# Rows of decay powers from one column by TensorE, first masks from the landed table, and a new order of low parts and conversions

## The chip, the cores and the metric

One core of one Trainium2 chip runs one program. The metric is the device time of one execution in microseconds (us). A trace by the hardware profiler belongs to one execution. Its engines are called PE (TensorE, the matrix products; PEld is its loading of weights), DVE (VectorE), ACT (ScalarE), POOL (GpSimd) and SP (SyncE, which issues most loads and stores).

## What is computed

Retention (attention with a decay) over 2 sequences of 768 positions with 8 heads of width 64, and behind it two feed-forward layers on 1536 tokens of width 512:

```python
Dmask = np.where(rel >= 0, lam[:, None, None] ** rel[None, :, :], 0.0)
lam_pow = lam[:, None, None] ** (pos[None, :, None] + 1)
for b in range(nb):
    intra = np.einsum('bhic,bhjc->bhij', qb, kb) * Dmask[None]
    intra = np.einsum('bhij,bhjd->bhid', intra, vb)
    inter = np.einsum('bhid,bhde->bhie', qb * lam_pow[None], kv_state)
    out[:, :, sl] = intra + inter
    kb_dec = kb * rev_pow[None]
    kv_state = lam_block[None, :, None, None] * kv_state + np.einsum('bhsd,bhse->bhde', kb_dec, vb)
# then, on the tokens:
x = np.maximum(x @ w_in, 0.0) ** 2 @ w_out
x = (1.0 / (1.0 + np.exp(-(x @ w_gate))) * (x @ w_val)) @ moe2_w_out
```

## The kernel before

The kernel works in chunks of 128 positions: chunks 0 to 5 are the first sequence, 6 to 11 the second, and a pair (c, c + 6) goes through the attention together. The order of the work on every engine is written out by hand (`tc.manual_schedule()`): each engine runs its instructions in the order of the program and waits where an operand or a buffer is not ready.

**The start.** `powers()` (L212) loads lam, makes the exponents `ex`, and POOL raises lam to them: `W` holds lam^1 to lam^128, one power a partition. `W` and zeros go to a table in memory, and `decay_table()` (L245) reads it back shifted by one row a partition, which gives every head's mask; its numbers lie eight apart. `warm_up(n)` (L268) issues n products that nothing uses. `state_decay()` (L232) picks the last power of each head into `G`, `decay_rows()` (L256) picks a row of the mask table for `L`, which scales queries; both by selecting products on TensorE with the matrix `E`. ScalarE and VectorE copy the table into `D` (L888, L889).

**The lead** (L898). For a pair: scores (L301, into two banks of PSUM a chunk; `sc`), the product of scores with the mask (L335, `at`, VectorE), keys and queries scaled by POOL (L322 `kd`, L310 `qd`), the new state's products (L368, `uv`), the output from within the chunk (L385) and from the state (L396), the update of the state `S` (L415, VectorE), its decay for the next pair (L352, ScalarE), and the output's copy or its split into a high and a low part (L425, L426). Four pairs go through the lead; the last two are put into slots of the following loop (`attend`, L810). The loads of q and k (`qk`), k and v (`kv`) and raw weights (`raw`) are issued by SP in the order of `FIRST`, `NEXT` and `LOOP`.

**The loop** `step_1(f)` (L828), f = 0 to 15, is the first layer on the first 512 tokens. TensorE does `stage_a(1, f)` (L457) and, a step later, `stage_b` (L471). Each weight comes as raw bits. It is converted in two operations on ScalarE (`conv_act`, L156 and L157) and three on VectorE (`conv_dve`: L179, L182, L174), of which the second reads the result of the first and the third that of the second. Then it is split into a high part (`whi`, ScalarE, L443) and a low part (`wlo`, VectorE, L445). `stage_a` needs the high part first and the low part from its fifth product on. The activations are split the same way (L498, L500). `weave(a, b)` issues two lists by turns, and `run` issues one. In most steps two weights are converted. Towards the loop's end `combine_x` and `combine_a` put more work on VectorE and ScalarE, for the products that follow it. Behind the loop come the rest of the first layer and the second layer; the change does not touch them.

Of the kernel before, what the change touches and what calls it, by code (L numbers as in the profile page):

```python
# [7 lines left out]
F32 = mybir.dt.float32  # L8
# [4 lines left out]
P = 128  # L13
CH = 128
TB = 512
WARM = 44
FILL = (72, 24)
# [22 lines left out]
def retention_moe_kernel(  # L40
# [40 lines left out]
    def bank():  # L81
        return ps.tile([P, 512], F32, tag="p", name="p")
# [120 lines left out]
    E = const.tile([P, 64], F32, name="E")  # L203
    G = [const.tile([P, 4, 1], F32, name=f"G{i}", tag=f"G{i}") for i in range(2)]
# [3 lines left out]
    L = [const.tile([P, 4, CH], F32, name=f"L{i}", tag=f"L{i}") for i in range(2)]  # L208
    S = [const.tile([P, 4, 64], F32, name=f"S{i}", tag=f"S{i}") for i in range(2)]
    w_dram = dram.tile([256, H], F32, name="w_dram")  # L210

    def powers():  # L212


        src = bass.AP(lam.tensor, lam.offset, [[0, P], [1, H]])
        nc.sync.dma_start(out=lam8, in_=src)
        nc.vector.memset(warm, 0.0)
        nc.gpsimd.iota(row, pattern=[[1, 1]], base=0, channel_multiplier=1)
        nc.vector.memset(Z[:, 0 : 127 * H], 0.0)
        nc.vector.memset(Z[:, 127 * H :], 1.0)  # L220
        nc.vector.tensor_scalar(out=ex, in0=row, scalar1=1.0, scalar2=None, op0=ALU.add)
        nc.vector.tensor_scalar(
            out=E, in0=row.to_broadcast([P, 64]), scalar1=127.0, scalar2=None, op0=ALU.is_equal
        )
        nc.scalar.dma_start(out=w_dram[0:128], in_=Z)
        nc.scalar.copy(ex, ex)
        nc.gpsimd.tensor_tensor(
            out=W[:, :, 0], in0=lam8, in1=ex.to_broadcast([P, H]), op=ALU.pow
        )
        nc.scalar.dma_start(out=w_dram[128:256], in_=W[:, :, 0])  # L230

    def state_decay():  # L232


        t = bank()
        w = W.rearrange("a (p r) o -> a r (p o)", r=2)
        for s in range(2):
            for g in range(2):
                nc.tensor.matmul(
                    t[64 * g : 64 * g + 64, 4 * s : 4 * s + 4], lhsT=E[64:128],  # L240
                    rhs=w[64:128, g ^ s], start=True, stop=True, skip_group_check=True,
                )
            nc.vector.tensor_copy(G[s][:, :, 0], t[:, 4 * s : 4 * s + 4])
# [11 lines left out]

    def decay_rows():  # L256


        for s in range(2):
            t = bank()  # L260
            for g in range(2):
                nc.tensor.matmul(
                    t[64 * g : 64 * g + 64], lhsT=E[64:128],
                    rhs=D[64:128, g ^ s].rearrange("a p i -> a (p i)"), start=True, stop=True,
                )
            nc.scalar.copy(L[s].rearrange("a p i -> a (p i)"), t)
# [47 lines left out]
    def att_prep(c):  # L314
        s, n = divmod(c, SEQ_CH)
        sc = sc_t.pop(c)
        at_t[c] = double("at")
        dst = [pv(at_t[c][:, g, :]) for g in range(2)]
        kn = kv_t[c][:, 0, :]
        if n < SEQ_CH - 1:  # L320
            kd = kd_t[c] = unit("kd")
            nc.gpsimd.tensor_tensor(  # L322
                out=kd.rearrange("s (h d) -> s h d", h=H),
                in0=kn.rearrange("s (h d) -> s h d", h=H),
                in1=W.to_broadcast([P, H, 64]), op=ALU.mult,
            )
        qt = qk_t.pop(c)[:, 0, :]
        if c == NCH - 1:
            query(NCH, qk_t.pop(NCH)[:, 0, :])
        elif c > SEQ_CH:  # L330
            query(c + 1, qk_t[c + 1][:, 0, :])
        elif 0 < n:
            query(c, qt)
        return [
            lambda g=g: nc.vector.tensor_tensor(  # L335
                out=dst[g], in0=pv(sc[g]), in1=D[:, g ^ s], op=ALU.mult
            )
            for g in range(2)
        ]
# [33 lines left out]
    def att_out(pair):  # L373
# [4 lines left out]
        for c in pair:  # L378
            s = c // SEQ_CH
            v = kv_t.pop(c)[:, 1, :].rearrange("s (h d) -> s h d", h=H)  # L380
# [22 lines left out]
        for c in pair:  # L403
            o_t[c] = uv_t.pop(c, None), ov[c]

    def att_state(c):
        s = S[c // SEQ_CH]
        uv, _ = o_t[c]
# [9 lines left out]
    def att_x(c):  # L418
        _, ov = o_t.pop(c)
# [390 lines left out]
    def attend(half):  # L810
# [7 lines left out]
        if what == "out":  # L818
# [4 lines left out]
            att_out(pair)  # L823
            passed(REST)
# [3 lines left out]
    def step_1(f):  # L828
# [3 lines left out]
        weave(conv_dve() if n > 0 else [], split_w(1, f + 1) if f + 1 < NF1 else [])  # L832
# [7 lines left out]
        weave(conv_dve() if n > 1 else [], ops)  # L840
# [31 lines left out]
    with tc.manual_schedule():  # L872
# [4 lines left out]
        state_decay()  # L877
# [10 lines left out]
        nc.scalar.copy(D[:, 0], table[:, 0])  # L888
        nc.vector.tensor_copy(D[:, 1], table[:, 1])  # L889
        ops = [op for c in PAIRS[0] for op in att_prep(c)]  # L890
        att_uv(PAIRS[0])
        warm_up(FILL[1])
        decay_rows()
        query(SEQ_CH + 1, qk_t[SEQ_CH + 1][:, 0, :])
        run(ops)
        for c in PAIRS[1]:
            att_scores(c)
        for k in range(LEAD):  # L898
# [3 lines left out]
            att_out(pair)  # L902
            if k + 2 < LEAD:
                for c in PAIRS[k + 2]:
                    att_scores(c)
# [12 lines left out]
            else:  # L918
                att_scores(PAIRS[LEAD][0])
                for c in pair:  # L920
                    run(att_state(c))
                run([f for c in pair for f in att_x(c)])
                weave(split_w(1, 0), ops)
# [106 lines left out]
```

## Time and profile before

| | us |
|---|---|
| median of 3 runs (lowest, highest) | 600.98 (599.19, 603.05) |
| the profiled execution: its time, its span | 600.89, 599.1 |
| busy in the span: PE, DVE, ACT, POOL | 583.8, 436.2, 339.6, 29.4 |

The span is the time from the first to the last instruction in the trace; around it lie 1.8 us. A wait stands in square brackets behind an instruction: how long its engine was idle and what it waited for. Matrix products overlap, so the distance from start to start tells more than a duration. [...]

### The profile page before, as it was taken

The numbers are of one execution on the slowest core, as the hardware profiler recorded it, in microseconds if no ns is written. First come the engines' busy times: TensorE is split into PE (matmuls) and PEld (weight loads), VectorE is DVE, ScalarE is ACT, GpSimd is POOL, SyncE is SP. The second block draws the span as 40 slices with busy tenths as digits, with TensorE's granted clock in tenths as the row PEclk, the third lists the DMA queues.
The fourth block names the chain that finished last, engine by engine and source line by source line (L and its number), as shares of the span: only waits on it lengthen the run. The fifth ranks groups of instructions, "written<-read, shape, count | busy, mean of one in ns | idle before, by whom it ended". The sixth has DMA issues, their size and how long they took to land.

```text
span 599.1 us, 8743 instructions
## 1 busy us (share of the span) xinstructions
PE 583.8 (97%) x3188; PEld 480.1 (80%) x3188; DVE 436.2 (73%) x676; ACT 339.6 (57%) x557; POOL 29.4 (5%) x29
## 2 busy tenths in 40 slices
PE   7898999998999999999999999999999999999997
PEld 7686778886788888888888888888888888888885
DVE  4359998899888868898977788694768676569101
ACT  3358888998656456666567654544454454537001
POOL 2471100000000000000000000000000000000000
PEclk9699999999999999999999999999999999999999
DMA  8995797793145376999988954511332422659003
GB/s 269 412 408 197 260 295 280 257 320 118 63 120 204 107 253 254 383 412 411 394 332 277 316 175 165 174 39 55 121 106 105 141 79 82 208 193 353 0 1 141
DMA packets 52157, 126.94 MB, mean 212 GB/s; under 512 B 5777, under 2 KB 6033, under 8 KB 52114
## 3 DMA queue, kind: packets, MB, share of 16 engines
q1 hardware_dynamic: 51024, 124.41, 57.9%
q10 hardware_dynamic: 1090, 1.97, 1.0%
q8 instruction: 25, 0.41, 0.3%
q14 instruction: 18, 0.15, 0.1%
HBM read 90.71 MB, written 35.66 MB: 211 GB/s over the span
## 4 chain that ended last, share of the span: by engine, by line
PE 82%; DVE 8%; ACT 4%; issue 3%; DMA 2%; POOL 0%; SPq 0%; ACTq 0%; DVEq 0%; POOLq 0%
PE p L623 30%; PE p L773 25%; PE p L457 13%; PE p L471 8%; PE p L301 2%; PE p L385 2%; DVE u L174 1%; DVE m L182 1%; DMA kv<-in_kv 1%; DVE t L556 1%; DMA a<-w 1%; DVE xcl L545 1%; PE p L396 1%; DVE m L179 1%; PE p L368 1%
## 5 line engine op out<-in xcount | busy, mean ns | idle before, releaser
L623 PE MATMUL p<-xch,ah 128*128 128x512 f32 x280 | 109.6, 392 | 0.2 <-DVE c L637 0.2
L623 PE MATMUL p<-xch,al 128*128 128x512 f32 x280 | 109.0, 389 | 0.0
L623 PE MATMUL p<-xcl,ah 128*128 128x512 f32 x280 | 109.0, 389 | 0.0
L773 PE MATMUL p<-g2h,whi 128*128 128x512 f32 x224 | 87.2, 389 | 0.0
L773 PE MATMUL p<-g2h,wlo 128*128 128x512 f32 x224 | 87.2, 389 | 0.0
L773 PE MATMUL p<-g2l,whi 128*128 128x512 f32 x224 | 87.2, 389 | 0.0
L623 PEld LDWEIGHTS p<-xch,ah 128*128 128x128 f32 x280 | 52.6, 188 | 13.1 <-ACT s L632 1.7
L623 PEld LDWEIGHTS p<-xch,al 128*128 128x128 f32 x280 | 52.6, 188 | 11.1
L637 DVE TENSOR_TENSOR c<-p,s 128x512 f32<-128x512 f32 x60 | 41.2, 688 | 27.5 <-PE p L623 21.0
L623 PEld LDWEIGHTS p<-xcl,ah 128*128 128x128 f32 x280 | 52.6, 188 | 10.7
L632 ACT COPY s<-p 128x512 f32<-128x512 f32 x60 | 35.2, 587 | 37.8 <-PE p L623 37.5
L156 ACT ACTIVATE j<-raw 128x512 f32<-128x512 f32 x68 | 45.8, 673 | 18.2 <-DMA raw<-in_w 10.4
L445 DVE TENSOR_TENSOR wlo<-u,whi 128x512 fp32r<-128x512 f32 x68 | 46.0, 704 | 7.3 <-ACT whi L443 6.0
L174 DVE CUSTOM_DVE_ANT_0 u<-m,r 128x1024 uint16<-128x1024 uint16 x68 | 48.6, 715 | 3.1
L773 PEld LDWEIGHTS p<-g2h,wlo 128*128 128x128 f32 x224 | 42.1, 188 | 8.8
L773 PEld LDWEIGHTS p<-g2h,whi 128*128 128x128 f32 x224 | 42.1, 188 | 8.7
L773 PEld LDWEIGHTS p<-g2l,whi 128*128 128x128 f32 x224 | 42.1, 188 | 8.7
L182 DVE SCALAR_TENSOR_TENSOR m<-j,m 128x512 int32<-128x512 int32 x68 | 47.9, 704 | 1.3
L457 PE MATMUL p<-xh,wlo 128*128 128x512 f32 x160 | 43.3, 393 | 4.8 <-DVE wlo L445 4.8
L157 ACT ACTIVATE r<-raw 128x512 int32<-128x512 uint32 x68 | 45.2, 664 | 4.5 <-PE p L471 2.9
L443 ACT CAST whi<-u 128x512 fp32r<-128x512 f32 x68 | 39.2, 617 | 12.2 <-DVE u L174 11.7
L457 PE MATMUL p<-xh,whi 128*128 128x512 f32 x160 | 43.1, 391 | 0.7 <-ACT whi L443 0.7
(98 smaller groups left out, 899.5 us busy)
## 6 DMA issues: line engine op xcount, KB each, us to landing
raw<-in_w SPq DMA_DIRECT2D x68, 512.0 KB, 7.0
w<-u SPq DMA_DIRECT2D x68, 256.0 KB, 4.0
u<-w SPq DMA_DIRECT2D x64, 256.0 KB, 5.0
g<-g SPq DMA_DIRECT2D x56, 256.0 KB, 4.3
g<-g SPq DMA_DIRECT2D x28, 512.0 KB, 7.7
a<-w SPq DMA_DIRECT2D x20, 512.0 KB, 4.0
kv<-in_kv SPq DMA_DIRECT2D x12, 512.0 KB, 9.2
qk<-in_qk SPq DMA_DIRECT2D x10, 512.0 KB, 8.7
```

The lines of the kernel that those rows point to most:

```text
L156: nc.scalar.activation(j, t[:, :, 1].bitcast(F32), AF.Copy, scale=2.0**-112)
L157: nc.scalar.activation(r, t[:, :, 0].bitcast(mybir.dt.uint32), AF.Copy, scale=2.0**-29)
L174: nc.vector.tensor_tensor(out=w.bitcast(I32), in0=m, in1=r, op=ALU.add)
L182: lambda: nc.vector.scalar_tensor_tensor(out=m, in0=j, scalar=-(2**31), in1=m, op0=ALU.bitwise_and, op1=ALU.bitwise_or),
L443: nc.scalar.copy(hi, src)
L445: lambda lo=lo, src=src, hi=hi: nc.vector.tensor_tensor(out=lo, in0=src, in1=hi, op=ALU.subtract)
L457: nc.tensor.matmul(acc, lhsT=a[:, kk * P : (kk + 1) * P], rhs=b[:, kk, :], start=i == 0, stop=i == 11,)
L471: nc.tensor.matmul(acc[e], lhsT=a[:, e * P : (e + 1) * P], rhs=b, start=first and i == 0, stop=last and i == 2,)
L623: nc.tensor.matmul(acc, lhsT=w[:, col, kk * P : (kk + 1) * P], rhs=x[:, kk, :], start=start and i == 0, stop=stop and i == 5, skip_group_c ...
L632: nc.scalar.copy(s, acc)
L637: nc.vector.tensor_tensor(out=c, in0=acc, in1=s, op=ALU.add)
L773: nc.tensor.matmul(acc[e, t], lhsT=a[:, e * P : (e + 1) * P], rhs=b[:, t, :], start=first and i == 0, stop=last and i == 2,)
```

## The change

- `E` and the selecting products go. `one` is a matrix with a single shifted diagonal of ones. Sixteen products with a column of `W`, repeated 64 times, as weights and `one` as the moving operand give the rows of powers; ScalarE copies them into `L` behind a first column of ones, which two writes have set. VectorE multiplies two columns of `L` for `G`. All this stands ahead of the first conversions.
- The masks of the first pair are multiplied with the landed table. Its copy to `D`, by ScalarE alone, comes behind that.
- In the lead the first pair's output comes ahead of the scores of the second pair, the first state's products come between these scores, and the number of warm-up products changes. The value tiles are held until both uses are through.
- At the lead's end the first weights' high parts are cast and their low parts made ahead of the outputs' casts and the conversion; in each step the low parts, and the activations' low part, come ahead of the conversion's three operations.

```diff
-FILL = (72, 24)
+FILL = (64, 40)
...
         nc.gpsimd.iota(row, pattern=[[1, 1]], base=0, channel_multiplier=1)
+        nc.gpsimd.iota(shift, pattern=[[1, CH]], base=0, channel_multiplier=-1)
+        for t in L:
+            nc.vector.memset(t[:, :, 0:1], 1.0)
         nc.vector.memset(Z[:, 0 : 127 * H], 0.0)
...
         nc.vector.tensor_scalar(
-            out=E, in0=row.to_broadcast([P, 64]), scalar1=127.0, scalar2=None, op0=ALU.is_equal
+            out=one, in0=shift, scalar1=1.0, scalar2=None, op0=ALU.is_equal
         )
...
+    def decay_rows():
         for s in range(2):
+            t = bank()
+            for p in range(4):
+                for g in range(2):
+                    nc.tensor.matmul(
+                        pv(t)[half(g), p, :],
+                        lhsT=W[:, 2 * p + (g ^ s)].to_broadcast([P, 64]), rhs=one,
+                        start=True, stop=True,
+                    )
+            nc.scalar.copy(L[s][:, :, 1:], pv(t)[:, :, 1:])
+            nc.vector.tensor_tensor(
+                out=G[s], in0=L[s][:, :, 1:2], in1=L[s][:, :, CH - 1 :], op=ALU.mult
+            )
...
-            v = kv_t.pop(c)[:, 1, :].rearrange("s (h d) -> s h d", h=H)
+            v = kv_t[c][:, 1, :].rearrange("s (h d) -> s h d", h=H)
...
         acc = stage_a(1, f)
-        weave(conv_dve() if n > 0 else [], split_w(1, f + 1) if f + 1 < NF1 else [])
+        run(split_w(1, f + 1) if f + 1 < NF1 else [])
+        run(conv_dve() if n > 0 else [])
...
-        weave(conv_dve() if n > 1 else [], ops)
+        run(ops)
+        run(conv_dve() if n > 1 else [])
...
         warm_up(WARM)
-        state_decay()
+        decay_rows()
...
         att_scores(6)
-        nc.scalar.copy(D[:, 0], table[:, 0])
-        nc.vector.tensor_copy(D[:, 1], table[:, 1])
-        ops = [op for c in PAIRS[0] for op in att_prep(c)]
-        att_uv(PAIRS[0])
         warm_up(FILL[1])
-        decay_rows()
+        for c in PAIRS[0]:
+            run(att_prep(c, table))
+        for r in range(2):
+            nc.scalar.copy(D[:, r], table[:, r])
         query(SEQ_CH + 1, qk_t[SEQ_CH + 1][:, 0, :])
-        run(ops)
-        for c in PAIRS[1]:
-            att_scores(c)
         for k in range(LEAD):
             pair = PAIRS[k]
             if k:
                 att_uv(pair)
             att_out(pair)
+            if not k:
+                att_scores(PAIRS[1][0])
+                att_uv(pair)
+                att_scores(PAIRS[1][1])
+            for c in pair:
+                kv_t.pop(c)
             if k + 2 < LEAD:
                 for c in PAIRS[k + 2]:
                     att_scores(c)
...
                 att_scores(PAIRS[LEAD][0])
+                late = split_w(1, 0)
                 for c in pair:
                     run(att_state(c))
-                run([f for c in pair for f in att_x(c)])
-                weave(split_w(1, 0), ops)
+                run(late + [f for c in pair for f in att_x(c)] + ops)
                 run(att_prep(PAIRS[LEAD][0]))
```

## Rows read from the trace of the kernel before

**Rows 1.** Stretches of the start: busy by engine (us), PEclk, DMA share, GB/s.
```profile
core 0: us, PE busy (x) PEld busy (x) DVE busy (x) ACT busy (x) POOL busy (x), PEclk, DMA share, GB/s
14.00:17.00 3.00, 0.15 (x4) 0.15 (x6) 2.05 (x4) 1.11 (x1) 1.04 (x1) 1.00 1.02 410
...
18.00:19.00 1.00, 1.00 (x14) 1.00 (x12) 0.06 (x1) 0.00 (x0) 0.00 (x0) 0.53 1.01 414
28.00:29.00 1.00, 1.00 (x20) 1.00 (x18) 0.36 (x1) 0.26 (x1) 1.00 (x2) 0.85 1.00 401
```

**Rows 2.** TensorE: scores at the low clock (timeline), a later pair (chain).
```profile
23.25 3.78 PE L301 MATMUL p<-qk 64*128 64x128 f32 x32
...
35.41 2.00 PE p L301 x32
37.41 1.08 PE p L368 x32
38.49 1.75 PE p L385 x32
40.24 1.04 PE p L396 x32
```

**Rows 3.** TensorE's timeline: start, us, and its waits for low parts of weights.
```profile
65.89 1.20 PE L457 MATMUL p<-xh,wlo 128*128 128x512 f32 x4 [0.73 <-DVE wlo L445]
...
144.75 1.21 PE L457 MATMUL p<-xh,wlo 128*128 128x512 f32 x4 [1.82 <-DVE wlo L445]
```

**Rows 4.** Issues of loads q9, q10, v9 (timeline); their us to landing (DMA issues).
```profile
14.79 0.44 SPq L119 DMA_DIRECT2D qk<-in_qk  x1
...
19.54 0.33 SPq L119 DMA_DIRECT2D qk<-in_qk  x1
...
24.62 0.33 SPq L123 DMA_DIRECT2D kv<-in_kv  x1
...
qk<-in_qk SPq DMA_DIRECT2D x1, 512.0 KB, 9.8
...
qk<-in_qk SPq DMA_DIRECT2D x1, 512.0 KB, 11.5
...
kv<-in_kv SPq DMA_DIRECT2D x1, 512.0 KB, 10.2
```

**Rows 5.** Timeline of the start: a small write, table's copies, first products.
```profile
1.93 0.07 DVE L220 MEMSET Z<- 1x8 f32 x1
...
14.43 1.11 ACT L888 COPY D<-decay 128x512 f32<-128x512 f32 x1 [3.42 <-DMA decay<-w_dram]
14.43 0.62 DVE L889 COPY D<-decay 128x512 f32<-128x512 f32 x1 [1.97 <-DMA decay<-w_dram]
15.57 2.48 DVE L335 TENSOR_TENSOR at<-p,D 128x512 f32<-128x512 f32 x4 [0.52 <-ACT D L888]
```

**Rows 6.** Timeline: state updates, order on VectorE, one operation of POOL, one cast.
```profile
30.73 1.28 POOL L310 TENSOR_TENSOR qd<-qk,L 128x512 f32<-128x512 f32 x1
...
41.31 0.76 DVE L415 TENSOR_TENSOR S<-p,tt 128x256 f32<-128x256 f32 x2 [1.00 <-PE p L396]
...
46.22 0.75 DVE L415 TENSOR_TENSOR S<-p,tt 128x256 f32<-128x256 f32 x2
...
48.09 0.42 DVE L179 TENSOR_SCALAR m<-j 128x512 int32<-128x512 int32 x1
48.42 0.69 DVE L445 TENSOR_TENSOR wlo<-u,whi 128x512 fp32r<-128x512 f32 x1
49.02 0.69 DVE L182 SCALAR_TENSOR_TENSOR m<-j,m 128x512 int32<-128x512 int32 x1
49.75 0.69 DVE L174 CUSTOM_DVE_ANT_0 u<-m,r 128x1024 uint16<-128x1024 uint16 x1
...
127.61 0.42 DVE L179 TENSOR_SCALAR m<-j 128x512 int32<-128x512 int32 x1
...
127.73 0.62 ACT L443 CAST whi<-u 128x512 fp32r<-128x512 f32 x1 [0.90 <-DVE u L174]
```

**Rows 7.** Two stretches of the loop; columns as in rows 1.
```profile
66.00:118.00 52.00, 52.00 (x378) 42.62 (x379) 47.38 (x81) 44.50 (x78) 4.79 (x4) 1.00 0.78 266
...
118.00:143.00 25.00, 23.92 (x104) 18.84 (x102) 24.28 (x41) 22.66 (x38) 0.00 (x0) 1.00 0.72 250
```

More of the change, by code (lines that the diff above doesn't have):

```diff
@@ L202, in retention_moe_kernel @@
     W = const.tile([P, H, 1], F32, name="W")
-    E = const.tile([P, 64], F32, name="E")
-    G = [const.tile([P, 4, 1], F32, name=f"G{i}", tag=f"G{i}") for i in range(2)]
+    shift = const.tile([P, CH], I32, name="shift")
+    one = const.tile([P, CH], F32, name="one")
     Z = double("Z").rearrange("a b c -> a (b c)")[0:1]
@@ L208, in retention_moe_kernel @@
     L = [const.tile([P, 4, CH], F32, name=f"L{i}", tag=f"L{i}") for i in range(2)]
+    G = [const.tile([P, 4, 1], F32, name=f"G{i}", tag=f"G{i}") for i in range(2)]
     S = [const.tile([P, 4, 64], F32, name=f"S{i}", tag=f"S{i}") for i in range(2)]
@@ L230, in powers @@
         nc.scalar.dma_start(out=w_dram[128:256], in_=W[:, :, 0])
-    def state_decay():
-        t = bank()
-        w = W.rearrange("a (p r) o -> a r (p o)", r=2)
+    def decay_rows():
         for s in range(2):
[L238 to L243, printed above, removed]
+            t = bank()
[10 more added lines that the diff above has]
+            )
     def decay_table():
@@ L254, in decay_table @@
         return t.rearrange("a b c -> a (b c)").rearrange("a (i p r) -> a r p i", p=4, r=2)
[L256 to L266, printed above, removed]
     def warm_up(n):
@@ L312, in query, with att_prep @@
         )
-    def att_prep(c):
+    def att_prep(c, table=None):
         s, n = divmod(c, SEQ_CH)
@@ L335, in att_prep @@
             lambda g=g: nc.vector.tensor_tensor(
-                out=dst[g], in0=pv(sc[g]), in1=D[:, g ^ s], op=ALU.mult
+                out=dst[g], in0=pv(sc[g]), in1=(D if table is None else table)[:, g ^ s], op=ALU.mult
             )
@@ L403, in att_out @@
         for c in pair:
-            o_t[c] = uv_t.pop(c, None), ov[c]
+            o_t[c] = ov[c]
     def att_state(c):
         s = S[c // SEQ_CH]
-        uv, _ = o_t[c]
+        uv = uv_t.pop(c, None)
         tt = tt_t.pop(c, None)
@@ L418, in att_x @@
     def att_x(c):
-        _, ov = o_t.pop(c)
+        ov = o_t.pop(c)
         blk, off = divmod(c * CH, TB)
@@ L902, in retention_moe_kernel @@
             att_out(pair)
+            if not k:
+                att_scores(PAIRS[1][0])
+                att_uv(pair)
+                att_scores(PAIRS[1][1])
+            for c in pair:
+                kv_t.pop(c)
             if k + 2 < LEAD:
```

## Prediction

> **What bounds the kernel now.** I read the table of stretches first, then TensorE's order of time, then the issues of loads with their times to landing, then VectorE's order of time. Everything that the change touches lies in the first 150 us. What follows is left as it is, and I take it to move along with whatever time TensorE reaches it.
>
> In that part the reader is to see two things. First, a slow start. [...] Second, from the end of the attention lead on it is VectorE that TensorE waits for: the low parts of weights release it at 65.89 and at 144.75 us [rows 3], and between 118 and 143 us VectorE is busy 24.28 of 25 us [rows 7].
>
> The loads bound the lead from below. By issue plus time to landing, chunk q9 is there at 14.79 + 9.8 = 24.6, q10 at 19.54 + 11.5 = 31.0, v9 at 24.62 + 10.2 = 34.8 us [rows 4]. The change leaves their order alone, and the 16 DMA engines stand at a share of 1.0 in these stretches [rows 1], so I keep these times.
>
> **The start, part by part.** Two small writes go ahead of the exponents on VectorE, on the way to the table's load. The nearest row is a write of 0.07 us, and a full-width operation takes 0.62 [rows 5]: 0.1 to 1.2 us for both. They cover four columns each, near the first, so I take **0.2 us, later** for every load behind the table.
>
> The products of the first pair then read the landed table instead of its copies. Four took 2.48 us from 15.57; now they start when the table lands (14.43, as both copies did) and end near 17.0 [rows 5]. The table has a stride of eight numbers: VectorE's copy of it took 0.62, ScalarE's 1.11 [rows 5]; at the dearer, the four end at about 19.
>
> On TensorE sixteen products for the rows of powers go in front. They have the shape of a pair's attention outputs, so 1.75 us [rows 2], and they replace the short selections and the long ones of the slow stretch. They run before the table is there, instead of warm-up. On ScalarE two copies of a bank (1.11 each at most, [rows 5]) now precede the first conversion and the issue of two loads. On POOL one more index row precedes the powers, while it waits for the exponents. One small product per sequence makes G. At the lead's end ScalarE casts the first weights (two casts of 0.62) ahead of the last outputs; the low part of f = 1, on VectorE, binds right behind, so I count that at nothing.
>
> The cover for all this is the wait for q9. From 17.0, TensorE has half an output of 0.9, scores 1.0, states 1.08, scores 1.0, scores 1.0: done at 22.0, and then it must wait until 24.6 + 0.2 [rows 2, 4]. So the start may be 2.6 us later at no cost, and beyond that each us costs one. The longer hold on key and value tiles and the banks taken by scores emitted early I cost at nothing on the same cover: eight banks suffice once the products of chunk 1 are through.
>
> **The lead.** The second pair's rest runs 1.0 + 1.08 + 1.75 + 1.04 = 4.9 us, from 24.6 to 29.5, and the next scores need q10 at 31.0. Then 1.0 (the half that needs it) + 1.08 + 1.75 + 1.04 = 4.9 more: the second state update of VectorE can start at 36.0 instead of 41.31. The step from it to the third update, 46.22 - 41.31 = 4.91 us, goes through ScalarE's decay, its casts and a conversion, none changed [rows 2, 6]. So the third stands at 40.95, **5.25 us earlier**. TensorE's own road does not take over: v9 at 34.8, two POOL operations of at most 1.28 each behind it, half the states, 1.75 + 1.04: 40.7 [rows 2, 4, 6].
>
> **The order on VectorE.** Here I see a price. Independent operations stand 0.33 (first conversion step) and 0.60 us apart, but the second step and the third, which reads its result, stand 0.73 apart: 0.13 more [rows 6]. Before, low parts were woven between the three steps of one of each two conversions, and one low part stood after the first step of the other. After the change all three stand together: two such pairs in each conversion, where there were none and one. That is 0.26 + 0.13 per step f. Also the second low part now comes right behind the first and waits for the cast of the weights that the last conversion has just made. That cast starts at the end of the conversion's last step and takes 0.62, the first low part takes 0.60, and its engine is free at 128.2 where the cast would end at 128.35: 0.2 us per step [rows 6]. In return the needed low part no longer has a first conversion step (0.33) in front of it.
>
> *Between 41 and 66 us* TensorE waits for low parts, so this shows. On the way to the wait at 65.89 lie five conversions, 2 x 0.26 + 3 x 0.13 = 0.91, and one wait of 0.2; the 0.33 comes off once: **0.8 us lost**. *Between 66 and 118* TensorE is busy 52.00 of 52 us and VectorE 47.38, so 4.6 us lie idle there [rows 7]. Nine steps or so at 0.26 + 0.13 + 0.2 cost 5.3: they fill that idle time and TensorE should feel nothing yet; what is left over, 0.7, makes the next stretch worse if anything. *Between 118 and 144* VectorE is full [rows 7]. Three woven and four other conversions lie there, 3 x 0.26 + 4 x 0.13 = 1.3, and three waits of 0.2, 1.9 in all: **2.0 us lost** at the wait of 144.75 [rows 3]. Its bounds are 0, if idle time between engines takes it up, and 2.7, if that 0.7 comes on top.
>
> [...]
>
> **Sum.** -5.25 + 0.8 + 2.0 + 0.2 = -2.2 us. The profiled execution took 600.89 us (span 599.1 and 1.8 around it), 0.1 off the median of 600.98, so **598.7 us**.
>
> **Rivals.** *The order on VectorE costs nothing:* slack takes up pairs and waits, and the 0.33 comes off. For it speaks that VectorE waited now and then even in the full stretch (0.7 of 25 us idle [rows 7]); against it that the two stalls of [rows 3] are waits for this engine. Then -5.25 - 0.3 + 0.2: 595.5 us. If the two stalls shrink beyond that, below 595.
>
> *The clock falls again, in the wait for q9* (this ends slower). Between about 21 and 24.7 us TensorE has only one chunk's scores to do, 1.0 of 3.6 us; the fall at 18 us followed a stretch of 0.15 in 3 [rows 1]. [...] Against it speaks that the stretch is partly busy.
>
> *A buffer or bank comes free late,* since key and value tiles are held past two uses and scores are emitted ahead of the products that free banks. In the lead nothing shows such a wait now. A load held by one landing costs up to 1.3 us, two or three of them more than the gain: 601 to 604 us, in a bad case more.
>
> **Chances.** Forecast, within 597 to 600.5 with a short fall of the clock in it: 0.5. Order free: 0.25. Long fall: 0.17. Late buffer or bank: 0.08. The range from 595.0 to 603.0 reaches to the free order and to the long fall. 1% of the median is 6.0 us, about what a measurement can tell from no change. Below 595.0 lies the far part of the free order, 0.11; above 607.0 the far part of the last two, 0.05; 0.84 stays within.
>
> **What would show it.** Right: no fall of the clock at 18 us; q9, q10 and v9 landing within 0.3 us of before; the third state update near 41; first products of step f = 0 near 42; waits for low parts at about 61 and at some 142 us, the later one larger than before by about 2 us; adjacent conversion steps 0.72 apart. Wrong on the lead: a clock of 0.50 behind 24 us, or the third update later than 42. Wrong on the order: PE's waits for low parts before 150 us in sum smaller than now.

## The result, and the profile after

| | us |
|---|---|
| changed kernel, median of 20 runs (lowest, highest) | 603.25 (601.81, 605.94) |
| kernel before, 20 runs beside them | 599.04 (597.15, 604.22) |
| ratio, 95% interval | 1.0061 [1.0041, 1.0081] |
| profiled execution of the changed kernel: its time, its span | 604.16, 602.4 |
| forecast, range | 598.7, 595.0 to 603.0 |

The change makes the kernel slower by 0.6%, where a small gain was forecast; the time lies just outside the range. Of the 20 runs of the kernel before, 8 took 600.9 us or more, with nothing between 599.2 and 600.9; against the mean of the other twelve (598.2) the changed kernel's mean (603.4) is 5.2 us longer. What sets the eight apart is b1's and b2's question, below. Line numbers of the changed kernel are lower by four from the loop on (L445 of before is L441).

First the start. The stretches, with the columns of [rows 1]:

```profile
12.00:15.00 3.00, 0.58 (x11) 0.41 (x8) 0.83 (x2) 0.00 (x0) 0.00 (x0) 0.93 0.97 315
15.00:18.00 3.00, 2.22 (x19) 2.00 (x20) 2.23 (x3) 2.19 (x2) 1.13 (x2) 0.50 1.03 422
18.00:21.00 3.00, 3.00 (x31) 3.00 (x30) 1.97 (x2) 0.00 (x0) 1.43 (x2) 0.50 1.02 416
21.00:24.00 3.00, 3.00 (x48) 2.73 (x48) 0.00 (x0) 0.00 (x0) 3.00 (x4) 0.94 1.03 411
```

The granted clock, which the profile gives as a share of full speed, still falls to 0.50 in this execution, now before 15 us and until 21.4. TensorE's timeline, of the lead and of all its waits between 48 and 156 us (start, us, and in brackets the idle time before and what ended it):

```profile
15.78 2.08 PE L297 MATMUL p<-qk 64*128 64x128 f32 x16 [3.20 <-DMA qk<-in_qk]
17.79 4.10 PE L268 MATMUL p<-warm 128*128 128x128 bf16 x40
21.82 1.97 PE L381 MATMUL p<-at,kv 128*64 128x128 f32 x32
...
40.95 1.75 PE L381 MATMUL p<-at,kv 128*64 128x128 f32 x28 [1.08 <-issue]
...
49.97 1.21 PE L453 MATMUL p<-xh,wlo 128*128 128x512 f32 x4 [1.29 <-DVE wlo L441]
63.89 1.20 PE L453 MATMUL p<-xh,wlo 128*128 128x512 f32 x4 [1.35 <-DVE wlo L441]
119.79 1.20 PE L467 MATMUL p<-gh,whi 128*128 128x512 f32 x4 [0.22 <-ACT gh L494]
126.48 1.20 PE L467 MATMUL p<-gh,whi 128*128 128x512 f32 x4 [0.88 <-ACT gh L494]
133.18 1.20 PE L467 MATMUL p<-gh,whi 128*128 128x512 f32 x4 [0.88 <-ACT gh L494]
138.90 1.21 PE L453 MATMUL p<-xh,wlo 128*128 128x512 f32 x4 [1.78 <-DVE wlo L441]
147.43 1.89 PE L453 MATMUL p<-xh,wlo 128*128 128x512 f32 x4 [2.20 <-DVE wlo L441]
```

The reader is to see two things. In the start TensorE now waits for a load, chunk q7 (second operand of the second scores), and forty warm-up products behind it run at the low clock. Before, its wait there was for keys scaled by POOL, not for the masks:

```profile
16.85 0.69 PE L368 MATMUL p<-kv,kd 128*64 128x64 f32 x16 [2.91 <-POOL kd L322]
```

And in the loop there are three waits that before did not have: for ScalarE's `gh`. ScalarE's timeline shows why q7 is late, the copies of the rows of powers ahead of the issues:

```profile
6.98 0.58 ACT L248 COPY L<-p 128x508 f32<-128x508 f32 x1 [2.92 <-PE p L243]
7.86 0.58 ACT L248 COPY L<-p 128x508 f32<-128x508 f32 x1 [0.29 <-PE p L243]
7.86 0.56 ACTq L119 DMA_DIRECT2D qk<-in_qk  x1
...
8.46 1.53 ACTq L119 DMA_DIRECT2D qk<-in_qk  x1
```

Their time to landing, and that of the table, which is issued at 9.49 (DMA issues; KB, us):

```profile
qk<-in_qk ACTq DMA_DIRECT2D x1, 512.0 KB, 7.3
...
decay<-w_dram SPq DMA_DIRECT2D x1, 512.0 KB, 6.1
```

VectorE's timeline: the first four products, the three state updates, and the order at the lead's end:

```profile
15.66 4.31 DVE L331 TENSOR_TENSOR at<-p,decay 128x512 f32<-128x512 f32 x4 [2.69 <-DMA decay<-w_dram]
...
32.74 0.76 DVE L411 TENSOR_TENSOR S<-p,tt 128x256 f32<-128x256 f32 x2 [1.79 <-PE p L392]
...
38.60 0.76 DVE L411 TENSOR_TENSOR S<-p,tt 128x256 f32<-128x256 f32 x2 [1.00 <-PE p L392]
...
43.77 0.76 DVE L411 TENSOR_TENSOR S<-p,tt 128x256 f32<-128x256 f32 x2 [0.17 <-PE p L392]
44.44 1.28 DVE L441 TENSOR_TENSOR wlo<-u,whi 128x512 fp32r<-128x512 f32 x2
...
46.24 0.42 DVE L179 TENSOR_SCALAR m<-j 128x512 int32<-128x512 int32 x1
46.70 0.69 DVE L182 SCALAR_TENSOR_TENSOR m<-j,m 128x512 int32<-128x512 int32 x1
47.42 0.69 DVE L174 CUSTOM_DVE_ANT_0 u<-m,r 128x1024 uint16<-128x1024 uint16 x1
```

The third update comes 2.45 us earlier than in [rows 6] (46.22), not 5.25. The two stretches of the loop, as in [rows 7], one behind them, ScalarE's waits between 50 and 146 us and VectorE's between 66 and 118 us (us in total, times, longest):

```profile
66.00:118.00 52.00, 52.00 (x378) 42.67 (x379) 47.13 (x78) 42.08 (x75) 4.27 (x4) 1.00 0.76 251
118.00:143.00 25.00, 21.24 (x87) 15.42 (x86) 23.89 (x39) 21.46 (x36) 0.00 (x0) 1.00 0.77 260
...
148.00:152.00 4.00, 4.00 (x13) 3.15 (x12) 3.96 (x4) 2.00 (x4) 0.00 (x0) 0.61 0.05 17
...
ACT whi L439 <- DVE u L174: 15.1, 11, 2.2
...
DVE gl L496 <- ACT gh L494: 2.7, 5, 0.8
```

TensorE loses 3.76 of the 25 us behind 118 us, against 1.08 before. VectorE is not busier than before (23.89 to 24.28, 47.13 to 47.38); ScalarE is less busy in the first stretch, 42.08 against 44.50, and does less work in the same time: it waits for VectorE, and VectorE in turn for it (2.7 us here, 2.8 before).

The whole loop can be measured in both traces, from the third update to the first product with `xch`, which stands behind the loop. Before, then after:

```profile
149.49 0.39 PE L623 MATMUL p<-xch,ah 128*128 128x512 f32 x1
```

```profile
153.70 0.39 PE L619 MATMUL p<-xch,ah 128*128 128x512 f32 x1
```

That is 103.3 us (from 46.22) and 109.9 us (from 43.77): 6.7 us more. The account of the two profiled executions: the first products of the step f = 0 start at 44.76 instead of 47.43, 2.7 us earlier; the waits between 48 and 148 us are 8.6 in sum instead of 4.85 (1.28 at 52.62, 1.02 at 136.94 and the two of [rows 3]), 3.75 us more; behind the last of them the clock stands at 0.50 for 3.4 us, worth 1.7; together +2.8 of the spans' difference of 3.3. That leaves out that the first four products behind a wait take some 0.13 us more than others, 1.04 from start to start instead of 0.91.

### The profile page after: what moved, and what is told of

Its sections match the earlier page's. It is cut to its first block, busy times and chain, and to the rows that moved or that the text cites. A ratio compares the mean times of both kernels' runs of the same rounds, so it can differ in the third digit from the quotient of the medians.

```text
span 602.4 us, 8777 instructions
## 1 busy us (share of the span) xinstructions
PE 583.9 (97%) x3212; PEld 481.2 (80%) x3212; DVE 441.3 (73%) x677; ACT 340.1 (56%) x558; POOL 28.7 (5%) x30
## 4 chain that ended last, share of the span: by engine, by line
PE 75%; DVE 5%; ACT 2%; issue 1%; ACTq 0%; DVEq 0%
PE p L619 32%; PE p L769 25%; PE p L453 11%; PE p L467 6%; DVE m L182 1%; DVE u L174 1%; DVE gl L496 1%; DVE xcl L541 1%; DVE wlo L441 1%; DVE m L179 0%; DVE t L552 0%; ACT r L157 0%; ACT g L485 0%; ACT gh L494 0%; ACT whi L439 0%
## 5 line engine op out<-in xcount | busy, mean ns | idle before, releaser
L619 PEld LDWEIGHTS p<-xcl,ah 128*128 128x128 f32 x280 | 52.6, 188 | 10.6
L441 DVE TENSOR_TENSOR wlo<-u,whi 128x512 fp32r<-128x512 f32 x68 | 45.0, 697 | 6.9 <-ACT whi L439 4.7
L453 PE MATMUL p<-xl,whi 128*128 128x512 f32 x160 | 43.7, 395 | 0.0
```

Of the source, the lines that this page charges most:

```text
L441: lambda lo=lo, src=src, hi=hi: nc.vector.tensor_tensor(out=lo, in0=src, in1=hi, op=ALU.subtract)
L453: nc.tensor.matmul(acc, lhsT=a[:, kk * P : (kk + 1) * P], rhs=b[:, kk, :], start=i == 0, stop=i == 11,)
L619: nc.tensor.matmul(acc, lhsT=w[:, col, kk * P : (kk + 1) * P], rhs=x[:, kk, :], start=start and i == 0, stop=stop and i == 5, skip_group_c ...
```

## Experiments

Two questions: which part of the change loses what the loop lost, and where the gain of the start went. All ratios are to the kernel before in the same comparison, with their 95% intervals. The fourth column is the kernel's mean less the mean of those executions of before, in the same comparison, whose mean granted clock was 0.994 or more (17 of 19 for x, 24 of 31 for y, 11 of 19 for z). The ratios count the others too, and so shift by their share. The last column is the loop's length in the trace, as above; an f says that the granted clock falls to 0.50 in it, for 3.4 us, worth some 1.7. Before has 103.3, the changed kernel 109.9 f.

| kernel | median us | ratio | to before at a high clock, us | loop, us |
|---|---|---|---|---|
| x1_order_only | 606.09 | 1.0132 [1.0097, 1.0168] | +7.8 | 110.0 f |
| x2_start_only | 598.69 | 1.0006 [0.9992, 1.0020] | +0.5 | 105.1 f |
| x3_side_first | 602.10 | 1.0071 [1.0056, 1.0086] | +4.1 | 109.9 f |
| x4_side_first_old_order | 596.84 | 0.9977 [0.9955, 0.9998] | -0.9 | 103.2 |
| y1_low_parts_first | 598.92 | 1.0005 [0.9984, 1.0025] | +1.0 | 105.4 |
| y2_low_products_first | 598.82 | 0.9990 [0.9967, 1.0014] | +0.9 | 105.3 f |
| y3_lead_end | 596.48 | 0.9971 [0.9948, 0.9994] | -1.2 | 103.3 |
| y4_conversion_first | 598.28 | 0.9995 [0.9975, 1.0014] | +0.3 | 104.7 |
| z1_copies_first | 597.97 | 0.9973 [0.9950, 0.9996] | -0.4 | 103.3 |
| z2_woven_then_products | 596.68 | 0.9948 [0.9927, 0.9968] | -1.4 | 103.4 |

**x1_order_only.** The kernel before, with the new order of VectorE in the loop and at the lead's end, and nothing else:

```diff
-        weave(conv_dve() if n > 0 else [], split_w(1, f + 1) if f + 1 < NF1 else [])
+        run(split_w(1, f + 1) if f + 1 < NF1 else [])
+        run(conv_dve() if n > 0 else [])
...
-        weave(conv_dve() if n > 1 else [], ops)
+        run(ops)
+        run(conv_dve() if n > 1 else [])
...
+                late = split_w(1, 0)
...
-                run([f for c in pair for f in att_x(c)])
-                weave(split_w(1, 0), ops)
+                run(late + [f for c in pair for f in att_x(c)] + ops)
```

> The kernel before with only the new order of low parts and conversions (steps of the loop and the lead's end); its start is the old one. Theory (the order is the loss): from the third state update to the end the changed kernel lost some 5.8 us against the one before, so this should be slower than before by 4.5 to 6 us, with new waits of TensorE for the activations' high part (gh) between 115 and 135 us, as in the changed kernel (0.22, 0.88, 0.88), and wlo waits near 140 and 148. Rival (the earlier start is paid back, since raw weights land no earlier): the order is nearly free, within 1 us of before, and no wait for gh.

Measured: 606.09, slower by 1.3%, with the three waits for `gh` (0.24, 0.89, 0.88) and, between 50 and 146 us, 15.4 us of waits of ScalarE for VectorE's `u`. The order alone brings all that is new in the loop. The loss is larger than either theory had it; the four executions had mean clocks of 0.986 to 0.997, and the profiled one has the slow start of [rows 1], so part of it is the clock.

**x2_start_only.** The changed kernel with the old order put back:

```diff
-        run(split_w(1, f + 1) if f + 1 < NF1 else [])
-        run(conv_dve() if n > 0 else [])
+        weave(conv_dve() if n > 0 else [], split_w(1, f + 1) if f + 1 < NF1 else [])
...
-        run(ops)
-        run(conv_dve() if n > 1 else [])
+        weave(conv_dve() if n > 1 else [], ops)
```

> The changed kernel with the old order of low parts and conversions; only its start is new. Theory (the order is the loss): the third state update near 43.8 as in the changed kernel, 2.45 us ahead of before, and all of it kept to the end: 2 to 3 us faster than before, no wait for gh. Rival (the earlier start is paid back): as slow as the changed kernel, some 3 to 4 us slower than before.

Measured: 598.69, the same as before, and neither theory's time. The third update stands at 44.23. The new start by itself gains nothing that shows; the waits for `gh` are gone, and those for low parts are the old ones (1.25, 0.73, 1.04, 1.82).

**x3_side_first** and **x4_side_first_old_order.** The changed kernel, and the same with the old order, with the loads of q6 and q7 issued ahead of the rows of powers:

```diff
+        load(SIDE, nc.scalar)
         decay_rows()
         new_xr()
         conv_act(False)
-        load(SIDE, nc.scalar)
```

> The changed kernel with ScalarE's issue of the loads q6 and q7 moved ahead of the rows of powers. Theory (those two loads stood behind ScalarE's copies, landed behind the table's neighbours at 15.7 instead of 12.1, and TensorE stood idle long enough for its clock to fall): q7 lands at 12 to 12.5, no granted clock of 0.50 at 14.5, scores of chunk 6 near 12.6, first outputs near 18 to 20 instead of 21.8, third state update 1.5 to 2.8 us earlier than the 43.77 of the changed kernel, 1.5 to 2.8 us faster than it in time. Rival (the table and its strided products, which end at 20, set the first outputs anyway): first outputs move by under 1.5 us, since the products still end near 19 to 20, and the time by under 1 us.

> Both mends: the loads issued ahead, and the old order. Theory: the sum, 4 to 5.3 us faster than before, near what the prediction gave for the lead alone (5.25). Rival (paid back): no faster than before.

Measured: 602.10 and 596.84. In both the wait for q7 shrinks, to 1.01 and 0.74 us (q7 is there at about 13.7 and 13.3, not at 12 to 12.5), and the clock stays at 1.00 through the start. With the old order the ratio goes from 1.0006 (x2) to 0.9977: the late loads cost about 1.7 us on average. Not every execution pays that: of x2's ten, four had a mean clock of 0.999 or 1.000 and took 597.2 to 598.4 us, the other six, at 0.991 to 0.994, 598.6 to 599.6. With the new order the trace gains as well, the third state update goes from 43.77 to 42.21, but the ratio, 1.0071, lies within the changed kernel's interval; against before at a high clock x3 loses 4.1 us where the changed kernel loses 5.2. Between x3 and x4, which differ in the order alone, lie 5.3 us: that is the price of the order. What x4 gains on the kernel before, 1.1 us, is far from the 4 or 5 that the profile of before had promised; that question is b2's, below.

**y1_low_parts_first, y2_low_products_first, y3_lead_end.** x4 with one part of the order each. In y1 the low parts of weights go ahead of the first conversion:

```diff
-        weave(conv_dve() if n > 0 else [], split_w(1, f + 1) if f + 1 < NF1 else [])
+        run(split_w(1, f + 1) if f + 1 < NF1 else [])
+        run(conv_dve() if n > 0 else [])
```

> x4 (the changed start with the loads of q6 and q7 issued ahead of the rows of powers, old order on VectorE; 596.84 in its own comparison) with one part of the new order: in each step f both low parts of weights ahead of the three conversion steps; the low part of the products stays woven in. Theory A (VectorE's step gets longer): two dependent neighbours at 0.46 and 0.73 instead of 0.34 and 0.60, and the second low part waits some 0.2 us for the cast of what the conversion has just made, 0.45 of the 0.55 us that a step of the new order is longer: most of the 5.3 us between x3 and x4, 600.5 to 601.5, waits for low parts of about 1.3 at 62 us and 2.2 at 145 us. Theory B (the low part of the products, placed ahead of a conversion, holds it up until ScalarE's gh is there, and this conversion is what ScalarE's next weight cast waits for): this part alone costs little, 596.5 to 598, and no wait of TensorE for gh.

In y2 the low part of the products goes ahead of the second conversion:

```diff
-        weave(conv_dve() if n > 1 else [], ops)
+        run(ops)
+        run(conv_dve() if n > 1 else [])
```

> x4 with the other part of the order alone: in each step the low part of the products ahead of the three steps of the second conversion, low parts of weights woven as before. Theory A: one dependent neighbour more, 0.11 us per step, 597 to 598. Theory B: the conversion queued behind the waiting low part comes later in each step, so ScalarE's casts and gh do; most of the 5.3 us, 600 to 602, with waits of TensorE for gh at 117, 124 and 130 us.

In y3 the lead's end is that of the changed kernel:

```diff
+                late = split_w(1, 0)
...
-                run([f for c in pair for f in att_x(c)])
-                weave(split_w(1, 0), ops)
+                run(late + [f for c in pair for f in att_x(c)] + ops)
```

> x4 with the third part alone: at the lead's end the low parts of the first weights ahead of the outputs' low parts and of the conversion. Both theories: the first wait for a low part, at 50 us, stays within 0.2 of 1.36 us and the time within 1 us of 596.8. A rival: the last chunks' outputs come later and the first step waits for them, up to 1 us slower.

Measured: 598.92, 598.82, 596.48; by the ratios +1.7, +0.8 and -0.4 us against x4. Together 2.1, where x3, which has all three, is 5.6 slower by the same measure. Differences of a few ratios carry much noise, but the loops say the same: against x4's 103.2, y1 takes 2.2 us more, y2 0.4 besides the fall of the clock, y3 0.1, and x3 5.0 besides that fall. Neither theory said that: y1 and y2 lie outside both ranges, and the parts together cost more than their sum. TensorE's waits for `gh` are 0.81 us in y1, 0.18 in y2 and 2.02 in x3. In y3 the first wait for a low part was 1.81 us, more than the 1.36 ± 0.2 expected. VectorE's own step agrees with the forecast's sum. Between two `xcl` in the stretch from 114 to 125 us (one step with all that it holds) lie 6.14 us in x4, 6.57 in y1, 6.27 in y2 and 6.70 in x3: 0.43 and 0.13 add up to 0.56. What does not add up is what TensorE feels.

**y4_conversion_first.** x3 with one exchange:

```diff
-        run(ops)
         run(conv_dve() if n > 1 else [])
+        run(ops)
```

> x3 (early loads, new order; 602.1) with one exchange: the three steps of the second conversion go ahead of the low part of the products, instead of behind it. All conversions still run with their steps adjacent, and the low parts of weights still come first. Theory A: VectorE's step stays as long as in x3 (nothing but the place of one operation of 0.6 us changes), so 601 to 602.5 with waits for gh at 117 to 131 us as in x3. Theory B: what ScalarE's second cast waits for comes before gh, the ring is cut, waits for gh are gone, 597 to 599.

Measured: 598.28, and no wait for `gh`. VectorE's step is 6.63 us, 0.07 short of x3's, so theory A, that the length of VectorE's step is what costs, falls; 4.5 us by the ratios come back by moving one operation, and 5.2 in the loop, 1.7 of them the clock's. The mechanism is seen when ScalarE and VectorE of x3 are read side by side. VectorE, then ScalarE, in x3:

```profile
118.81 0.68 DVE L496 TENSOR_TENSOR gl<-g,gh 128x512 fp32r<-128x512 f32 x1
119.41 0.42 DVE L179 TENSOR_SCALAR m<-j 128x512 int32<-128x512 int32 x1
119.86 0.69 DVE L182 SCALAR_TENSOR_TENSOR m<-j,m 128x512 int32<-128x512 int32 x1
120.59 0.69 DVE L174 CUSTOM_DVE_ANT_0 u<-m,r 128x1024 uint16<-128x1024 uint16 x1
121.20 1.46 DVE L441 TENSOR_TENSOR wlo<-u,whi 128x512 fp32r<-128x512 f32 x2
...
121.32 0.62 ACT L439 CAST whi<-u 128x512 fp32r<-128x512 f32 x1 [0.53 <-DVE u L174]
...
124.26 0.62 ACT L494 CAST gh<-g 128x512 fp32r<-128x512 f32 x1
```

The weight `u` is the last thing that VectorE makes in a step, 0.6 us later than it need be because `gl` stands in front. ScalarE's second cast waits for it, and everything queued behind that cast on ScalarE waits too: the next conversion, then relu, square and the cast `gh`, which starts 2.94 us behind. TensorE needs `gh` first of all in its second half of a step, `gl` last. In the new order VectorE's lateness is handed through ScalarE to what TensorE needs soonest; with the exchange it falls on `gl`, which can be late longest. y4 shows the same debt in its new place, two waits of TensorE for `gl`, 0.93 us at 53.27 and 2.10 at 139.59. ScalarE's waits for the weight, same view as above, in x3's neighbours x4, y1, y2, y4:

```profile
ACT whi L439 <- DVE u L174: 10.8, 11, 2.0
```

```profile
ACT whi L439 <- DVE u L174: 13.7, 12, 2.4
```

```profile
ACT whi L439 <- DVE u L174: 13.7, 11, 2.1
```

```profile
ACT whi L439 <- DVE u L174: 10.7, 12, 1.7
```

They rise with the loss, 10.8, 13.7, 13.7 and 15.1 (x3) as the order is taken over piece by piece, and with the exchange fall back to 10.7. They do not measure it: y4's loop is still 1.5 us longer than x4's.

**z2_woven_then_products.** The best of these put together: y3 (early loads, low parts woven, new lead's end) with the exchange of y4:

```diff
-        weave(conv_dve() if n > 1 else [], ops)
+        run(conv_dve() if n > 1 else [])
+        run(ops)
```

> y3 with one exchange in the loop: low parts of weights woven into the first conversion as before, the second conversion's three steps all ahead of the low part of the products. If ScalarE's wait for the weight that this conversion makes sets the pace of the loop (10.7 us of such waits between 50 and 146 us in y4 and 10.8 in x4, 15.1 in x3), both savings add up: waits of ScalarE near 9 us, 595 to 596. If VectorE is simply full, one more adjacent pair per step makes it 597 to 598, and the low part of the products comes late for TensorE (2.1 us at 139.59 in y4).

Measured: 596.68, above the 595 to 596 hoped for; the ratio, 0.9948, is the lowest of all and below both kernels. The waits of ScalarE for the weight are 9.2 us, near the 9 expected, and TensorE's waits for `gl` and the low parts between 50 and 160 us are down to 2.9:

```profile
PE p L467 <- DVE gl L496: 1.9, 2, 1.5
PE p L453 <- DVE wlo L441: 1.0, 2, 0.5
...
ACT whi L439 <- DVE u L174: 9.2, 9, 2.0
```

Against the changed kernel the gain is 1.1%. Against y3 none is shown: the ratios differ by 0.23%, which the intervals do not separate, against before at a high clock it is 1.4 to 1.2 us, and the loops are equally long (103.4 and 103.3). So the exchange that won back most of the loss on the new order brings nothing on the woven one, and less waiting of ScalarE for the weight (9.2 us against y3's 10.6) does not by itself make the loop shorter.

**z1_copies_first.** y3 with the first four products reading copies of the table, as before:

```diff
-        for c in PAIRS[0]:
-            run(att_prep(c, table))
-        for r in range(2):
-            nc.scalar.copy(D[:, r], table[:, r])
+        nc.scalar.copy(D[:, 0], table[:, 0])
+        nc.vector.tensor_copy(D[:, 1], table[:, 1])
+        for c in PAIRS[0]:
+            run(att_prep(c))
```

> y3 (start of the change with early loads, old order in the loop, new order at the lead's end; 596.48, third state update 41.74) with the first four products reading copies of the table again, as in the kernel before, instead of the landed table with its stride. The four took 4.11 us from 14.54 in y3 and 2.48 from 15.57 before. If the strided reads bind the start, they now end near 18.0 instead of 18.65, the first outputs come 0.6 us sooner and the time is 595.6 to 596.3. If the loads or TensorE's own road through the lead bind, nothing changes: 596.2 to 597.

The products in y3 and in z1:

```profile
14.54 4.11 DVE L331 TENSOR_TENSOR at<-p,decay 128x512 f32<-128x512 f32 x4 [1.46 <-DMA decay<-w_dram]
```

```profile
15.71 2.49 DVE L331 TENSOR_TENSOR at<-p,D 128x512 f32<-128x512 f32 x4 [0.54 <-ACT D L887]
```

From the strided table one costs 1.03 us, from the copy 0.62; waiting for the copies, the four end at 18.20 instead of 18.65. The ratio is the same, 0.9973 to 0.9971, though z1's median, 597.97, lies above both ranges; the loops are equal, and the third update stands at 42.21, 0.47 later than in y3. So copies gain nothing there, and the strided reads do not bind. "First masks from the landed table" brings little on the early loads, at most the 0.8 us between z1 and y3 against before at a high clock, which is near the noise: what it saves by not waiting for the copy it pays in dearer reads.

**b1_before_again, b2_before_again.** The kernel before, unchanged, for two more traces. The reason lies in the runs: of 50 executions of before beside the x and y kernels, 41 took 596.8 to 600.3 us with a mean granted clock of 0.994 or more, the other nine 601.1 to 602.6 with 0.988 or 0.991. The execution that the prediction read had 0.991. In the other comparisons the long executions are more: 8 of 19 beside the z kernels (600.9 to 602.5, 0.988 or 0.991), and the 8 of 20 beside the changed kernel, whose clocks are not on record; in all 25 of 89.

> The kernel before, unchanged, for a second trace. The prediction took the start of one execution (mean granted clock 0.991 over the span, clock at 0.50 from 18 to 28 us, third state update at 46.22) as the kernel's own. Theory A: most executions of before do not lose these ten us of clock; with a mean clock of 0.997 or so the span is near 596, the low clock at the start lasts 4 us or less, and the third state update stands at 42.5 to 44: then most of the 5.25 us of the forecast was not there to be gained. Theory B: the slow start belongs to every execution, third state update at 46 to 47.5, and the change's gain was lost elsewhere.

> The kernel before, unchanged, for a third trace. The second one again had a low mean clock (0.988, third state update at 47.48), though most timed executions stand at 0.994 to 0.999 and 597 to 599 us. If the mean clock of this execution is 0.994 or more, theory A (the low clock at the start is what sets those apart) has the third state update at 42.5 to 44.5 and the first products of the step f = 0 below 45.5; theory B has them at 46 to 47.5 as in the first two traces, and the difference of 4 us elsewhere.

Measured: b1 took 602.19 us at 0.988, third update at 47.48; b2 took 597.99 at 0.997. b2's start, and its state updates:

```profile
15.00:18.00 3.00, 0.98 (x23) 0.91 (x24) 2.47 (x5) 0.66 (x1) 1.04 (x1) 1.00 1.03 418
18.00:21.00 3.00, 3.00 (x31) 1.51 (x28) 0.18 (x1) 0.59 (x1) 0.00 (x0) 1.00 1.03 421
...
31.19 0.76 DVE L415 TENSOR_TENSOR S<-p,tt 128x256 f32<-128x256 f32 x2 [3.48 <-PE p L396]
37.05 0.76 DVE L415 TENSOR_TENSOR S<-p,tt 128x256 f32<-128x256 f32 x2 [1.00 <-PE p L396]
42.68 0.75 DVE L415 TENSOR_TENSOR S<-p,tt 128x256 f32<-128x256 f32 x2
```

TensorE does the same work with the same gaps as in [rows 1] (its longest wait is 3.13 us, where the trace that was read has 2.91), and the clock stays at 1.00: the scores that took 3.78 us [rows 2] take 2.46, the rows of powers 1.93 instead of 3.68, and the third update stands at 42.68, 3.5 us earlier than in the profile that was read. Theory A holds. By their times and clocks, 64 of the 89 executions were like b2: in most the slow start was not there to be removed. That it sets all 25 others apart is concluded from three traces, the one that was read, b1 and b2. Against b2 the changed kernel's third update, 43.77, is 1.1 us later; that of y3, 41.74, is 0.9 earlier.

## Why the prediction was wrong

Two terms of its sum failed. The lead's -5.25 us: the new start alone measured +0.5 us against before at a high clock (x2). Of the term, 3.5 us were a fall of the clock that most executions do not have, and the late loads turned the rest into a loss. And the order's 0.8 + 2.0 us: it measured 4.7 to 5.0, and 6.7 in the trace with the clock that falls behind it; 2.0 of that are waits of TensorE for ScalarE's `gh`, which the prediction did not follow.

**Its base.** "600.89 us ..., 0.1 off the median of 600.98": the one trace and the median of three runs agreed, and both lay in the slower part of what the kernel does; the 89 runs beside other kernels have a median of 598.45. Of the 5.25 us that the start was to gain, 3.5 were a fall of the clock that this execution had and most do not. That is the largest part of the failure, and the profile gave a hint that was not weighed: the mean granted clock was 0.991, and the argument rested on a stretch that held nearly all of the missing part (0.50 to 0.51 from 18 to 27 us and 0.78 from 27 to 30, 5.1 us of the 5.4 that are missing in 599.1). No run shows what made the clock fall: between 18 and 21 us b1 and b2, the same program, have 0.50 and 1.00.

**The start's cover.** The step that failed here is the one sentence on ScalarE: two copies "now precede the first conversion and the issue of two loads". It was priced on ScalarE and not followed to the loads. They are issued at 7.86 and 8.46 instead of 6.64 and 7.23, q7 lands near 15.8, and the table, issued 1.0 us behind the second of them where it was 2.8 before, takes 6.1 us (4.3 before). TensorE waits 3.20 us for q7, and in the profiled execution the clock falls. The first output starts at 21.82 where the slack allowed 19.6; of the 4.8 us behind the forecast's 17.0 the slack took 2.6, and 2.2 are left; the second and third update stand at 38.60 and 43.77, 2.6 and 2.8 us behind the forecast. x3 shows that by its opposite: with the loads early the clock stays up and the third update comes 1.56 us earlier.

**The products from the table** were sized at the cheaper bound, 0.62 us each; they took 1.08 here and 1.03 in y3, the dearer (1.11). ScalarE's copy of the table is dear too (1.11, against 0.58 for one of a bank); VectorE's copy of the same table, 0.62 [rows 5], is not, and no run shows what sets the price. z1 shows that the error cost nothing where the loads are early.

**The lead behind it** was right in its pace. Forecast 29.5, 36.0 and 40.95 for the first outputs' end and the two updates; y3, whose start is not held up, has its updates at 29.56, 35.85 and 41.74. Its TensorE runs through from 19 us on with gaps of at most a few tenths and one of 0.59 us for which the trace shows no cause (1.08 at 40.95 in the changed kernel). By issue plus time to landing q9, q10 and v9 are there at 24.2, 30.7 and 34.5 in y3 and at 24.5, 31.8 and 35.7 in the changed kernel, whose SP goes on issuing at 15.58, when the table has landed, as it does at 14.42 before, against 24.6, 31.0 and 34.8. The lead's end at nothing: y3, -0.4 us by the ratios, right.

**The order on VectorE.** The sizes were right: neighbours that depend on each other stand 0.46 and 0.72 apart, as said, and a step grows by 0.56 us (x4 to x3) where 0.13, 0.26 and 0.2 gave 0.59. The wait at 63.89 grew by 0.62 where 0.8 was forecast. What failed is "TensorE should feel nothing yet" and the single term of 2.0 us behind 118. The 5.3 us were to fill VectorE's idle time; but most of that time was not free: in 2.8 of the 4.6 us VectorE stood still for ScalarE's `gh`, and the new order makes that `gh` later, so VectorE's busy time in the stretch did not rise at all (47.13 to 47.38 of 52). In place of 2.0 us at one wait stand 1.98 us of new waits for `gh`, 0.76 and 0.38 more at the two last waits for low parts, 3.1 in sum, and 1.7 for the clock that falls behind the wait of 2.20. That fall is not the order's alone: with the loop's old order b2 and x2 have it behind a wait of 1.82 us, while before and x4 (clock at 1.00) and, by their lengths, y3 and z1 (103.3 us) and b1 (552.9 us from the third update to the end, as before) do not. No rival named ScalarE.

**The rivals.** The free order falls (x1, x3). The clock did fall, but not by that rival's way: it fell in the wait for q7, not for q9, and was back at 21.4. No run shows a long fall in the wait for q9; one at 18 us was measured on the kernel before, at 3.5 us by the third update (46.22 in the trace that was read, 42.68 in b2). A late buffer or bank shows nowhere in the lead, unless the gap without a shown cause is one.

**In sum**, against before at a high clock: the change +5.2 us, the start with its late loads +0.5 (x2), so the order on top of it 4.7. On the early loads the order costs 5.0 (x4 to x3). The ratios make it 3.3 (1.0061 to 1.0006) and 5.6 (1.0071 to 0.9977), as if the late start hid some of it; but 8 of the 20 executions of before beside the changed kernel were long ones, and 2 of the 19 beside x2 to x4. The loop's length shows that nothing is hidden: 109.9 us in the changed kernel, 109.9 in x3 and 110.0 in x1, whatever the start, all three with the fall of the clock. With the old order it is 103.2 or 103.3 without the fall, and 104.9 (b2) and 105.1 (x2) with it. So the order costs about 5 us on every start, and the fall 1.6 to 1.9 more. Whether the longer last wait makes the fall more frequent is not shown.

## What to carry to other kernels

Before a stretch with a low clock is counted as something to gain, compare the mean granted clock of the profiled execution with that of the other runs: here the one that was read had 0.991 and 41 of the 50 beside the x and y kernels 0.994 or more, so that in most there was no such fall to remove. The same holds for a ratio of means: where executions with a fall are more frequent on one side, it carries their share, and the length of the stretch in the traces is the better measure. Idle time of an engine is slack only if it does not wait there for the very engine that the edit delays; follow each result made later to the queue that it heads, and to what stands behind it there. And of two operations that one engine has to do, put first the one on which another engine's queue stands still, not the one that is ready or looks nearest to the end; where that queue was not what TensorE waited for (y3 to z2), the same exchange brought nothing.

## What had not been expected of the hardware

- The same program with the same gaps kept its clock in one execution (1.00 at 18 to 21 us in b2, after 0.98 us of work in 3) and lost it in others (0.51 in the execution that was read and 0.50 in b1, in the same stretch). A wait of 1.8 us in the loop was followed by a fall in x2 and b2 and not in x4.
- A product of a PSUM bank with a table of stride eight took 1.02 to 1.08 us on VectorE against 0.62 with a packed one.
- Where ScalarE's two loads were issued 1.2 us later (the changed kernel), the table's transfer, 512 KB issued 1.0 us behind the second of them on the other queue, took 6.1 us (6.7 in x2); with the loads early (x3) it took 4.3, as before.
- In every trace of the new start TensorE stands still for 0.4 to 1.1 us in the last outputs of the lead with nothing shown that it waits for; this was left open.
